# Loading an expert's first layer from memory for each block, in a kernel of polynomial attention and a cosine router

## The chip, the cores and the metric

The kernel runs on one core of a Trainium2 chip. TensorE (PE in the profile, with its weight loads as PEld), VectorE (DVE), ScalarE (ACT), GpSimd (POOL) and SyncE (SP) each work through an instruction list of their own and wait for each other by semaphores. The metric is the device time of one execution in microseconds.

## The reference

Attention without a softmax: queries and keys are turned into 64 features each, and the output is a ratio of two products. Its result, 4352 rows of 128, goes into a router that sends every row to one of 8 experts.

```python
a, b = S1 @ x, S2 @ x                    # 8 numbers each
phi(x) = outer(a, b).reshape(64)
kv = sum over s of phi(k)[f] * v[d];  z = sum over s of phi(k)
x = (phi(q) @ kv) / (phi(q) @ z + 1e-6)  # heads side by side: (4352, 128)

logits = normalised(x) @ normalised(expert_emb).T / tau
expert_idx = argmax(logits);  gate_w = softmax(logits)[expert_idx]
for e in range(8):
    mask = expert_idx == e
    h = maximum(x[mask] @ w1[e], 0)      # 128 -> 1024
    out[mask] = gate_w[mask] * (h @ w2[e])  # 1024 -> 128
```

All is in float32. w1 and w2 have 8 x 128 x 1024 and 8 x 1024 x 128 numbers, 4 MB each.

## The kernel before

The batch of 4 is worked in two halves (m = 0 and 1), each in groups of four token tiles and one last tile. For each group `keys` builds the key features (`tr`, `ab`, `b`, `prod`, `kv`) and `queries` the query features and the output (`tr`, `ab`, `b`, `prod` or `prods`, `tr_qp`, `qpT`, `nd`, `x`); in the first half the query features are kept in `held` until kv is known. `router` finds the best expert of each row (`best`, `pick`), its place among the rows of that expert (`place`, `take`, `split`, `mark`), and writes the rows with their logits to `rows` in memory (`write`, L682 and L686, by SP).

The rows are then worked in blocks of 128 that each have one expert. `plan_early` lays out the first 10 blocks from the counts of the first half, `plan_late` the others from all counts (`count`, `rest`, `shared`, `others`, `experts`); `table` turns places into lists of row numbers (`find`, `high`, `low`, `sums`, `tokens`). Four blocks (30 to 33) have two experts, 64 rows each. 36 blocks are always worked, two more only if a count asks for it (the branch at L1095).

A block i is worked as: `fetch` (POOL gathers its rows, L881), `norm` (ACT squares and sums, POOL takes the root, L949 and L950), `inverse` (DVE, L953 and L954), `turn` (PE transposes the rows, ACT or DVE copies them to xT, L887 and L889), `weights` (the expert's first layer is copied from `w1_sb` to `wb`, L893), `up` (PE, 16 matmul passes, L936, and ACT's relu to hT, L944), `shares` and `share` (the gate, L960, L963, L964), `down` (PE with the second layer, L972 or L975; ACT scales to y, L978; POOL scatters y to the output, L981). Which expert a block has is known only as the program runs: it stands as a number in `exp_i`, an engine loads it into a register (L897), and the address is made from it.

Both layers of all experts are loaded into SBUF by SP: `w1_sb` whole (L181), `w2_sb` for two experts at once and for the others in stages (L176), since its upper half serves as `held`. In w1 as loaded, the 1024 columns stand in the order of memory; the copy to `wb` reorders them so that PE can take 128 at a time.

The order of all work is written out by hand. `put(after, rank, f)` files a step under a tick and a rank, and `emit` issues the steps in that order, on every engine, SP and POOL too. Block i's `up` is in tick first + i (L1061), where first is 10; a step with a lower rank comes sooner in its tick. Buffers rotate: `wb` has four (the tag "rows", shared with the first k and q tiles), xT two, `norm` four, `xs` six, the large PSUM tiles (`ps_big`) two. SP's transfers go by eight semaphores in turn.

POOL is drained once (L1091, ahead of `up` of block 32): it waits there until all that it was given is finished.

Of the kernel before, what the change touches and what calls it, by code (L numbers as in the profile page):

```python
# [19 lines left out]
P = 128  # L20
# [43 lines left out]
def kernel(  # L64
# [113 lines left out]
    LATER = 6  # L178
# [304 lines left out]
    def queries(m, c0, c1, put, put_nd):  # L483
# [52 lines left out]
        def tr_qp():  # L536
            ps = ps_big() if n > 1 else ps_small().rearrange("p (b n) -> p b n", b=2)
            for j in range(n):
# [3 lines left out]
            s["ps"] = ps[:, :, :w]  # L542

        def qpT():
            s["qpT"] = tile_of(n, [P, 2, w], "qpT")
            nc.scalar.copy(s["qpT"], s["ps"])
# [42 lines left out]
        else:  # L589
# [5 lines left out]
                       {tr: (8, 55.3), ab: (8, 84.6), b: (8, 84.7), prod: (9, 20.2), tr_qp: (9, 30.2), qpT: (9, 30.6),  # L595
# [5 lines left out]
        if c1 == s1:  # L601
# [92 lines left out]

    exp_i = [consts.tile([1, n], I32, name=f"exp_i{i}") for i, n in enumerate((EARLY, LATE + SHARED))]

    def blocks(which, upto, weight, place):
# [12 lines left out]

        def experts():
            f = consts.tile([1, n], F32, name=f"exp_f{which}")
            nc.vector.reduce_sum(out=f[:], in_=le[0:1], axis=AX.X)
            nc.vector.tensor_scalar_min(exp_i[which], f, float(E - 1))
        return first, experts
# [60 lines left out]
    def plan_early():  # L776
# [6 lines left out]
        def rest():  # L783
            nc.vector.tensor_tensor_scan(out=upto[:], data0=ones_e[:], data1=full[:], initial=0.0, op0=ALU.mult, op1=ALU.add)
            nc.vector.tensor_scalar(w, full, -1.0, float(KEYS), op0=ALU.mult, op1=ALU.add)
            first, early["experts"] = blocks(0, upto, w, lane)
# [4 lines left out]
        def others():  # L791
            early["experts"]()

# [5 lines left out]
    def plan_late():  # L799
# [12 lines left out]
        def rest():  # L812
# [11 lines left out]
            late["first"], _ = blocks(1, upto, w_late, place)  # L824
# [60 lines left out]
    def turn(i):  # L885
        ps = ps_small()
        nc.tensor.transpose(ps[:, :P], xs[i][:, :DM], ident)  # L887
        xT[i] = w2_sb[:, LATER, 0] if i == 0 else work.tile([P, P], F32, tag="xTb", name="xTb")
        (nc.scalar.copy if i == 0 or 4 <= i <= 8 else nc.vector.tensor_copy)(xT[i], ps[:, :P])  # L889

    def first_layer(to, e, copy=nc.vector.tensor_copy):

        copy(to.rearrange("p (f q) -> p f q", f=NF),  # L893
                              w1_sb[:, bass.ds(e, 1)].rearrange("p o (q f) -> p (o f) q", f=NF))

    def expert(t, j, engine):
        return nc.values_load(exp_i[t][0:1, j:j + 1], engines=(engine,), min_val=0, max_val=E - 1,  # L897
                              skip_runtime_bounds_check_because="a count of experts, clamped to the last one")

    def weights(i):  # L900
        e = expert(*of(i), mybir.EngineType.Activation if i == 0 else mybir.EngineType.DVE)
        wb[i] = rows_p.tile([P, F], F32, tag="rows", name="wb")
        first_layer(wb[i], e, nc.scalar.copy if i == 0 else nc.vector.tensor_copy)
# [11 lines left out]
    def weights_b(i):  # L915
        first_layer(first_b(i), expert(1, LATE + i - FULL, mybir.EngineType.DVE))
# [121 lines left out]
    put(0, 75.5, count)  # L1038
# [17 lines left out]
    def in_ticks(b0, b1, tick):  # L1056
        for i in range(b0, b1 + 1):
# [33 lines left out]
    put_at(first + USUAL - AHEAD)(0, 29.5, lambda: nc.gpsimd.drain(fusable=False))  # L1091
# [42 lines left out]
```

## Time and profile before

| | us |
|---|---|
| median of 3 runs | 212.22 (211.96 to 213.15) |
| the profiled execution | 211.64 |
| its span, first to last instruction | 209.9 |
| PE busy | 194.9 (93% of the span) |
| DVE, ACT, POOL busy | 133.8, 104.0, 118.9 |
| granted TensorE clock | full, in all slices |
| first layer's matmuls start, block 0 | 56.84 |
| the same, blocks 3, 10 and 35 | 74.77, 104.61, 199.96 |
| first gather starts, lands | 52.56, 55.80 |

The profile is of one execution; its sums stand against 211.64, and the 1.7 us around the span are outside of it. A line of the timeline has start and length in us, engine, line of the program, operation, the tile written and those read, and in brackets the idle time of the engine in front of it with whoever ended it. Busy time of PE counts pipelined matmuls with modelled ends.

### The profile page before, as it was taken

To read this page: it belongs to the slowest core of one execution; us is meant where nothing else is said; L and a number is where in the kernel's file an instruction comes from. 1 tells how busy PE (TensorE), PEld (TensorE's weight loads), DVE (VectorE), ACT (ScalarE), POOL (GpSimd) and SP (SyncE) were. 2 spreads that over 40 slices of the span, in tenths; PEclk is the share of its full clock that TensorE was granted. 3 is DMA by queue.
4 is the path that set the end of the run, shared out by engine and by line. 5 is a ranking of instruction groups with operands and counts; after the bars stand their busy time and mean duration, and the time that the engine had idled before them with its cause. 6 is when DMAs were issued, how large, how long until landed. Compare 5 with 4: busy or idle time off the path is not lost.

```text
span 209.9 us, 6913 instructions
## 1 busy us (share of the span) xinstructions
PE 194.9 (93%) x2598; PEld 184.1 (88%) x2598; DVE 133.8 (64%) x441; ACT 104.0 (50%) x292; POOL 118.9 (57%) x134
## 2 busy tenths in 40 slices
PE   8999899989679889999999999999999999999881
PEld 7668798977569889999999999999999999999781
DVE  5867578979877858898536554646464456784220
ACT  2566432353573425652346555454655545777430
POOL 4101000210852757964788888888888888881533
PEclk9999999999999999999999999999999999999999
DMA  4988889998164140100111111111111121110000
GB/s 122 310 209 286 250 294 391 355 384 319 48 179 171 47 128 23 42 16 13 42 41 44 38 39 41 39 41 29 41 33 37 43 41 41 31 40 5 10 25 24
DMA packets 18560, 22.64 MB, mean 108 GB/s; under 512 B 5353, under 2 KB 12788, under 8 KB 18528
## 3 DMA queue, kind: packets, MB, share of 16 engines
q1 hardware_dynamic: 16224, 17.45, 24.8%
q0 software_dynamic: 2304, 4.74, 8.7%
q8 instruction: 22, 0.36, 0.7%
q14 instruction: 10, 0.08, 0.1%
HBM read 17.59 MB, written 4.73 MB: 106 GB/s over the span
## 4 chain that ended last, share of the span: by engine, by line
PE 62%; DVE 17%; issue 8%; POOL 5%; DMA 3%; ACT 2%; DVEq 0%; POOLq 0%
PE ps_big L936 20%; PE ps_acc L972 9%; PE ps_ab L972 9%; PE ps_big L941 4%; PE ps_acc L437 3%; DMA xs<-rows,src_i 3%; PE ps_t L357 2%; POOL out_dram L981 2%; POOL norm L950 2%; PE ps_acc L103 2%; PE ps_t L887 2%; PE ps_acc L975 2%; PE ps_big L554 2%; PE ps_big L520 2%; PE ps_ab L374 2%
## 5 line engine op out<-in xcount | busy, mean ns | idle before, releaser
L981 POOL DMA_INDIRECT out_dram<-y,dst_i x36 | 48.6, 1350 | 29.4 <-ACT sq L949 17.7
L936 PE MATMUL ps_big<-xTb,wb 128*128 128x128 f32 x496 | 61.1, 276 | 3.6 <-DVE xTb L889 1.2
L936 PEld LDWEIGHTS ps_big<-xTb,wb 128*128 128x128 f32 x496 | 57.8, 192 | 4.6 <-issue 3.1
L944 ACT ACTIVATE hT<-ps_big 128x1024 f32<-128x1024 f32 x36 | 36.9, 1024 | 39.9 <-PE ps_big L936 38.8
L881 POOL DMA_INDIRECT xs<-rows,src_i x36 | 39.6, 1100 | 19.5 <-DVE rc L565 9.7
L893 DVE COPY wb<-w_sb 128x1024 f32 x35 | 38.7, 1104 | 12.2 <-issue 11.1
L972 PE MATMUL ps_acc<-w_sb,hT 128*128 x256 | 31.3, 275 | 0.0
L972 PE MATMUL ps_ab<-w_sb,hT 128*128 x256 | 31.2, 275 | 0.0
L972 PEld LDWEIGHTS ps_ab<-w_sb,hT 128*128 128x128 f32 x256 | 29.9, 192 | 0.0
L972 PEld LDWEIGHTS ps_acc<-w_sb,hT 128*128 128x128 f32 x256 | 29.8, 192 | 0.0
L950 POOL TENSOR_TENSOR norm<-norm,half_c 128x1 f32<-128x1 f32 x36 | 25.9, 722 | 2.5 <-ACT sq L949 1.9
L953 DVE TENSOR_SCALAR norm<-norm 128x1 f32<-128x1 f32 x36 | 5.5, 152 | 27.2 <-POOL norm L950 27.1
L960 ACT ACTIVATE probs<-xs,norm 128x8 f32<-128x8 f32 x36 | 10.7, 296 | 7.1 <-DVE norm L954 5.5
L390 POOL TENSOR_TENSOR qp<-both 128x1024 f32<-128x1024 f32 x1 | 2.0, 1958 | 21.4 <-ACT both L385 21.4
L889 DVE COPY xTb<-ps_t 128x128 f32<-128x128 f32 x30 | 8.6, 287 | 6.8 <-PE ps_t L887 6.5
L978 ACT ACTIVATE y<-ps_ab,gate 128x128 f32<-128x128 f32 x18 | 6.6, 366 | 12.7 <-PE ps_ab L972 10.9
L390 DVE TENSOR_TENSOR kp<-ps_ab,kb 128x1024 f32<-128x1024 f32 x8 | 9.7, 1215 | 3.9 <-ACT qpT L529 2.4
L887 PE MATMUL ps_t<-ident,xs 128*128 128x128 f32 x36 | 10.2, 283 | 2.0 <-DMA xs<-rows,src_i 2.0
L978 ACT ACTIVATE y<-ps_acc,gate 128x128 f32<-128x128 f32 x18 | 6.6, 367 | 10.9 <-PE ps_acc L972 8.0
L949 ACT ACTIVATE sq<-xs 128x128 f32<-128x128 f32 x36 | 10.8, 300 | 0.1
L437 PEld LDWEIGHTS ps_acc<-v,kp 128*64 128x64 f32 x256 | 8.1, 138 | 1.8 <-issue 1.7
L437 PE MATMUL ps_acc<-v,kp 128*64 128x64 f32 x256 | 9.2, 225 | 0.3 <-issue 0.3
(241 smaller groups left out, 308.4 us busy)
## 6 DMA issues: line engine op xcount, KB each, us to landing
w_sb<-in_moe_w_dram SPq DMA_DIRECT2D x32, 256.0 KB, 5.7
rows<-xg SPq DMA_DIRECT2D x4, 544.0 KB, 5.0
v<-in_v_dram SPq DMA_DIRECT2D x4, 512.0 KB, 7.2
k<-in_k_dram SPq DMA_DIRECT2D x3, 512.0 KB, 5.2
q<-in_q_dram SPq DMA_DIRECT2D x3, 512.0 KB, 6.4
xs<-rows,src_i POOLq DMA_INDIRECT x36, 2.6
out_dram<-y,dst_i POOLq DMA_INDIRECT x36, 2.3
k<-in_k_dram SPq DMA_DIRECT2D x2, 256.0 KB, 2.9
```

Source lines behind the costliest of these rows:

```text
L390: engine.tensor_mul(t.rearrange("p j h (i k) -> p (j h) i k", i=R), ab[:, :, 0].unsqueeze(3).broadcast_to([P, n * H, R, R]), b.unsqueeze(2 ...
L437: nc.tensor.matmul(acc[m][u * HALF:(u + 1) * HALF, i, p], s["kp"][:, c - c0, h], bass.AP(tensor=vo.tensor, offset=vo.offset, ap=[list(vo.a ...
L881: nc.gpsimd.indirect_dma_start(out=xs[i][:], out_offset=None, in_=rows[:2 * S if t == 0 else N], in_offset=bass.IndirectOffsetOnAxis(ap=sr ...
L887: nc.tensor.transpose(ps[:, :P], xs[i][:, :DM], ident)
L893: copy(to.rearrange("p (f q) -> p f q", f=NF), w1_sb[:, bass.ds(e, 1)].rearrange("p o (q f) -> p (o f) q", f=NF))
L936: nc.tensor.matmul(ps[:, u, j * P:(j + 1) * P], w[:, f * P:(f + 1) * P], x, start=True, stop=True)
L944: nc.scalar.activation(hT[i], ps, ACT.Relu)
L949: nc.scalar.activation(sq, xs[i][:, :DM], ACT.Square, accum_out=norms[i])
L950: nc.gpsimd.tensor_tensor(out=norms[i], in0=norms[i], in1=half_c, op=ALU.pow)
L972: nc.tensor.matmul(ps, h[:, f * P:(f + 1) * P], ws[0][:, f], start=f == 0, stop=f == NF - 1)
L978: nc.scalar.activation(y, ps, ACT.Copy, scale=gate.pop(i)[:, 0:1])
L981: d = nc.gpsimd.indirect_dma_start(out=out[:, :], out_offset=bass.IndirectOffsetOnAxis(ap=dst_i[t][:, j:j + 1], axis=0), in_=y[:], in_offs ...
```

## The change

`w1_sb` is gone. `first_layer` now loads the expert's whole first layer, 128 rows of 4 KB, from memory into `wb` (or into the free halves of `v_flat` for the second expert of a block) by SP, with the expert's number in a register of SP. There is no copy, on DVE or, for block 0, on ACT; columns come in memory's order, and w2 is loaded in the matching order ("(f p) d" for "(p f) d"), in pieces of 512 bytes where it was 2048. All of w2 is loaded at once behind the attention's inputs, since `held` is a tile of its own.

The number of block 0's expert is made first and alone (`expert_0`, into `exp_0`), the other nine in a later tick. The transposes of one query group are issued in two halves, with `turn(0)` between them. `norm` is issued three blocks ahead where it was two, with six buffers; that of block 0 stands ahead of its `up`, that of the last block ahead of the drain. The late counts, and with them the place of the last group's rows, stand behind `up` of block 3 where they stood ahead of it. POOL is drained once more, in the middle of the blocks (before `up` of block 18).

```diff
-    w1_sb = consts.tile([P, E, F], F32, name="w1_sb")
-    held = w2_sb[:, E // 2:].rearrange("p e f d -> p e (f d)")
+    held = consts.tile([P, E // 2, F], F32, name="held")
     def load_w2(e):
         for u in range(2):
-            nc.sync.dma_start(w2_sb[:, e, f], w2[e].rearrange("(p f) d -> p f d", p=P)[:, f])
+            nc.sync.dma_start(w2_sb[:, e, f], w2[e].rearrange("(f p) d -> p f d", p=P)[:, f])
     for e in range(E):
-        for u in range(2):
-            nc.sync.dma_start(w1_sb[:, e, u * F // 2:(u + 1) * F // 2], w1[e, :, u * F // 2:(u + 1) * F // 2])
-    for e in range(2):
         load_w2(e)
...
-                       {..., tr_qp: (9, 30.2), qpT: (9, 30.6),
+                       {..., (lambda: tr_qp(0)): (9, 30.2), (lambda: tr_qp(1)): (9, 30.22), qpT: (9, 30.6),
...
-                at_rank = {best: (1, 31), pick: (1, 31), place: (1, 75.1), take: (1, 76), split: (1, 76),
+                at_rank = {best: (1, 31), pick: (1, 31), place: (2, 31), take: (2, 32), split: (2, 32),
...
+        def expert_0():
+            nc.vector.reduce_sum(out=f[:], in_=le[0:1], axis=AX.X)
+            nc.vector.tensor_scalar_min(exp_0, f[:, 0:1], float(E - 1))
         def experts():
-            nc.vector.reduce_sum(out=f[:], in_=le[0:1], axis=AX.X)
             nc.vector.tensor_scalar_min(exp_i[which], f, float(E - 1))
...
-    def first_layer(to, e, copy=nc.vector.tensor_copy):
-        copy(to.rearrange("p (f q) -> p f q", f=NF),
-                              w1_sb[:, bass.ds(e, 1)].rearrange("p o (q f) -> p (o f) q", f=NF))
+    def first_layer(to, t, j):
+        e = expert(t, j, mybir.EngineType.SP)
+        nc.sync.dma_start(to, w1[bass.ds(e, 1)].rearrange("o p f -> (o p) f"))
...
-        norms[i] = work.tile([P, 1], F32, tag="norm", bufs=4, name="norm")
+        norms[i] = work.tile([P, 1], F32, tag="norm", bufs=6, name="norm")
...
-    for e in range(2, LATER):
-        put_at(ND_AT[0][-1])(0, 55.5 if e < 4 else 83, lambda e=e: load_w2(e))
-    for e in range(LATER, E):
-        put_at(ND_AT[0][-1])(3, 30.1, lambda e=e: load_w2(e))
...
+    put(0, 62.2, lambda: early["expert_0"]())
+    put(1, 21, lambda: early["experts"]())
-    put(1, 30.1, lambda: turn(0))
+    put(1, 30.21, lambda: turn(0))
...
-    put(0, 75.5, count)
+    put(1, 31.5, count)
...
-                known_by = i - (1 if EARLY <= i <= known + AHEAD else 2) - b0
-                to = put_at(tick + max(known_by, 0))
-                to(*((0, 46) if i == b0 else (0, 74.6)), lambda i=i: norm(i))
-                to(*((0, 59) if i == b0 else (1, 46)), lambda i=i: inverse(i))
+                t = max(i - (1 if EARLY <= i <= known + AHEAD else 3), b0)
+                to = put_at(tick + t - b0)
+                if i == 0:
+                    put(-1, 30.7, lambda: norm(0))
+                    put(0, 59, lambda: inverse(0))
+                else:
+                    to(0, 46 if i == b0 else 29.2 if i == USUAL - 1 else 74.6, lambda i=i: norm(i))
+                    to(*((1, 46) if i > t else (0, 59)), lambda i=i: inverse(i))
...
-    put_at(first + USUAL - AHEAD)(0, 29.5, lambda: nc.gpsimd.drain(fusable=False))
+    for t in (USUAL // 2, USUAL - AHEAD):
+        put_at(first + t)(0, 29.5, lambda: nc.gpsimd.drain(fusable=False))
```

More of the change, by code (lines that the diff above doesn't have):

```diff
@@ L175, in load_w2 @@
             f = slice(u * NF // 2, (u + 1) * NF // 2)
-            nc.sync.dma_start(w2_sb[:, e, f], w2[e].rearrange("(p f) d -> p f d", p=P)[:, f])
-    LATER = 6
+            nc.sync.dma_start(w2_sb[:, e, f], w2[e].rearrange("(f p) d -> p f d", p=P)[:, f])
     for e in range(E):
-        for u in range(2):
-            nc.sync.dma_start(w1_sb[:, e, u * F // 2:(u + 1) * F // 2], w1[e, :, u * F // 2:(u + 1) * F // 2])
-    for e in range(2):
         load_w2(e)
@@ L534, in prods, with tr_qp @@
                                  s["b"][:, j].rearrange("p (j a n) -> p j a n", j=2, a=2))
-        def tr_qp():
-            ps = ps_big() if n > 1 else ps_small().rearrange("p (b n) -> p b n", b=2)
-            for j in range(n):
+        def tr_qp(half=None):
+            if half != 1:
+                s["ps"] = ps_big() if n > 1 else ps_small().rearrange("p (b n) -> p b n", b=2)
+            ps = s["ps"]
+            for j in range(n) if half is None else range(2 * half, 2 * half + 2):
                 for p in range(2):
@@ L541, in tr_qp @@
                                         s["qp"][:, j, 2 * p:2 * p + 2].rearrange("p h f -> p (h f)"), ident)
-            s["ps"] = ps[:, :, :w]
         def qpT():
             s["qpT"] = tile_of(n, [P, 2, w], "qpT")
-            nc.scalar.copy(s["qpT"], s["ps"])
+            nc.scalar.copy(s["qpT"], s["ps"][:, :, :w])
         def nd():
@@ L594, in queries @@
                         nd: (9, 30), x: (9, 71)},
-                       {tr: (8, 55.3), ab: (8, 84.6), b: (8, 84.7), prod: (9, 20.2), tr_qp: (9, 30.2), qpT: (9, 30.6),
+                       {tr: (8, 55.3), ab: (8, 84.6), b: (8, 84.7), prod: (9, 20.2), (lambda: tr_qp(0)): (9, 30.2),
+                        (lambda: tr_qp(1)): (9, 30.22), qpT: (9, 30.6),
                         nd: (10, 70), x: (10, 71)},
@@ L693 @@
     dst_i = [consts.tile([P, n], I32, name=f"dst_i{i}") for i, n in enumerate(SIZES)]
+    exp_0 = consts.tile([1, 1], I32, name="exp_0")
     exp_i = [consts.tile([1, n], I32, name=f"exp_i{i}") for i, n in enumerate((EARLY, LATE + SHARED))]
@@ L709, in first @@
             return at
+        f = consts.tile([1, n], F32, name=f"exp_f{which}")
+        def expert_0():
+            nc.vector.reduce_sum(out=f[:], in_=le[0:1], axis=AX.X)
+            nc.vector.tensor_scalar_min(exp_0, f[:, 0:1], float(E - 1))
         def experts():
-            f = consts.tile([1, n], F32, name=f"exp_f{which}")
-            nc.vector.reduce_sum(out=f[:], in_=le[0:1], axis=AX.X)
             nc.vector.tensor_scalar_min(exp_i[which], f, float(E - 1))
-        return first, experts
+        return first, expert_0, experts
     def column(name, dt=F32, w=E):
@@ L785, in rest @@
             nc.vector.tensor_scalar(w, full, -1.0, float(KEYS), op0=ALU.mult, op1=ALU.add)
-            first, early["experts"] = blocks(0, upto, w, lane)
+            first, early["expert_0"], early["experts"] = blocks(0, upto, w, lane)
             at = first()
@@ L791, in others @@
         def others():
-            early["experts"]()
             nc.vector.tensor_scalar_min(c_early[:, 1:], upto, float(EARLY))
@@ L823, in rest @@
             nc.vector.tensor_add(place[:, PAIRS:PAIRS + SHARED], place[:, PAIRS:PAIRS + SHARED], s["high"])
-            late["first"], _ = blocks(1, upto, w_late, place)
+            late["first"], _, _ = blocks(1, upto, w_late, place)
         def shared():
@@ L887, in turn @@
         nc.tensor.transpose(ps[:, :P], xs[i][:, :DM], ident)
-        xT[i] = w2_sb[:, LATER, 0] if i == 0 else work.tile([P, P], F32, tag="xTb", name="xTb")
+        xT[i] = work.tile([P, P], F32, tag="xTb", name="xTb")
         (nc.scalar.copy if i == 0 or 4 <= i <= 8 else nc.vector.tensor_copy)(xT[i], ps[:, :P])
-    def first_layer(to, e, copy=nc.vector.tensor_copy):
-        copy(to.rearrange("p (f q) -> p f q", f=NF),
-                              w1_sb[:, bass.ds(e, 1)].rearrange("p o (q f) -> p (o f) q", f=NF))
     def expert(t, j, engine):
-        return nc.values_load(exp_i[t][0:1, j:j + 1], engines=(engine,), min_val=0, max_val=E - 1,
+        number = exp_0[:, 0:1] if t == j == 0 else exp_i[t][0:1, j:j + 1]
+        return nc.values_load(number, engines=(engine,), min_val=0, max_val=E - 1,
                               skip_runtime_bounds_check_because="a count of experts, clamped to the last one")
+    def first_layer(to, t, j):
+        e = expert(t, j, mybir.EngineType.SP)
+        nc.sync.dma_start(to, w1[bass.ds(e, 1)].rearrange("o p f -> (o p) f"))
     def weights(i):
-        e = expert(*of(i), mybir.EngineType.Activation if i == 0 else mybir.EngineType.DVE)
         wb[i] = rows_p.tile([P, F], F32, tag="rows", name="wb")
-        first_layer(wb[i], e, nc.scalar.copy if i == 0 else nc.vector.tensor_copy)
+        first_layer(wb[i], *of(i))
     def second_layer(t, j):
@@ L915, in weights_b @@
     def weights_b(i):
-        first_layer(first_b(i), expert(1, LATE + i - FULL, mybir.EngineType.DVE))
+        first_layer(first_b(i), 1, LATE + i - FULL)
     def second_b(i):
```

## The prediction

> **What bounds the kernel now.** I read the 40 slices first, then busy times by window, then the chain of waits and the timeline where TensorE (PE) has holes.
>
> The slices: a digit is the busy tenths of 5.25 us.
>
> ```profile
> PE   8999899989679889999999999999999999999881
> ...
> DMA  4988889998164140100111111111111121110000
> ```
>
> PE is full except around slices 11 to 15, 18 to 20 and the end; DMA is full until 50 us and nearly empty afterwards. By window (start:end, length, then busy us of PE, its weight loads, DVE, ACT, POOL):
>
> ```profile
> 50.00:55.00 5.00, 3.61 (x69) 3.13 (x67) 4.51 (x17) 3.01 (x2) 2.13 (x2) 1.00 0.43 152
> 55.00:60.00 5.00, 4.20 (x58) 4.03 (x58) 3.93 (x7) 2.71 (x7) 3.55 (x4) 1.00 0.20 48
> 60.00:65.00 5.00, 3.83 (x41) 3.35 (x39) 3.58 (x16) 2.73 (x11) 2.64 (x4) 1.00 0.88 293
> 70.00:75.00 5.00, 3.33 (x47) 3.08 (x46) 4.15 (x20) 1.96 (x6) 4.48 (x6) 1.00 0.43 149
> ...
> 115.00:190.00 75.00, 75.00 (x835) 74.31 (x835) 43.15 (x131) 42.55 (x126) 63.89 (x63) 1.00 0.15 38
> ```
>
> From 105 to 195 us PE never idles: a block costs 1.79 (first layer) + 1.79 (second) + about 0.1 = 3.69 us, and nothing there can gain. The holes are 1.39 + 0.80 + 1.17 + 1.67 us in these windows, 0.85 between 90 and 105, and one at the end. Who ended them (start, length, in brackets the idle time and its releaser):
>
> ```profile
> 55.80 0.33 PE L887 MATMUL ps_t<-ident,xs 128*128 128x128 f32 x1 [1.82 <-DMA xs<-rows,src_i]
> 60.83 0.15 DVE L953 TENSOR_SCALAR norm<-norm 128x1 f32<-128x1 f32 x1 [0.68 <-POOL norm L950]
> 62.61 2.02 PE L936 MATMUL ps_big<-xTb,wb 128*128 128x128 f32 x16 [1.17 <-DVE parts L570]
> 74.77 2.02 PE L936 MATMUL ps_big<-xTb,wb 128*128 128x128 f32 x16 [0.96 <-DVE place_k L669]
> 93.88 2.02 PE L936 MATMUL ps_big<-xTb,wb 128*128 128x128 f32 x16 [0.32 <-DVE wb L893]
> 96.29 2.17 PE L748 MATMUL ps_t<-col,row 128*128 128x64 bf16 x34 [0.38 <-DVE col L742]
> 197.69 0.15 DVE L953 TENSOR_SCALAR norm<-norm 128x1 f32<-128x1 f32 x1 [4.47 <-POOL norm L950]
> 199.96 2.05 PE L936 MATMUL ps_big<-xTb,wb 128*128 128x128 f32 x16 [1.19 <-DVE xTb L889]
> ```
>
> Nearly all are PE behind DVE, and DVE behind its copies or behind POOL's norm. The groups that the change touches:
>
> ```profile
> L893 DVE COPY wb<-w_sb 128x1024 f32 x35 | 38.7, 1104 | 12.2 <-issue 11.1
> L981 POOL DMA_INDIRECT out_dram<-y,dst_i x36 | 48.6, 1350 | 29.4 <-ACT sq L949 17.7
> L950 POOL TENSOR_TENSOR norm<-norm,half_c 128x1 f32<-128x1 f32 x36 | 25.9, 722 | 2.5 <-ACT sq L949 1.9
> ```
>
> **What the Trainium skill says.** "SBUF — State Buffer", section "SBUF: two separate sides": DMA ports and engine ports don't contend, while GpSimd and some DVE operations lock each other out for a whole instruction. The trace agrees on the lock: the norm at 70.32 lasts 1.45 us and ends at 71.77, just behind the copy at 70.64 (1.10); a free one takes 0.58. An output scatter takes 1.49 us over a copy and 1.02 clear of one. "DMA: Bandwidth & Descriptors", section "Specifications", gives 512 B as the least transfer for line rate; the trace's packet records have 27 ns for 512 B and 84 ns for 2048 B, on 16 engines 303 against 390 GB/s. Its section "Latency and other measured facts" gives a register load about 600 ns; the trace has 0.70 (DVE, 64.60) and 0.51 (POOL, 206.03).
>
> **Copies out, loads in.** 39 DVE copies go (35 for wb, 4 for v; 38.7 + 4.4 us) with 0.33 to 0.88 us of register load before each, and one ACT copy (2.09). In their place SP issues 40 loads of 512 KB (36 blocks, 4 second halves). Transfer: 4096-byte packets are not in this queue's trace; between 84 ns for 2048 and 168 for 4352 I take 160, so 8 packets an engine are 1.3 us of 3.69. Time to landing: the 544 KB row writes at 63.29 and 72.18, in a quiet queue, took 2.76 and 3.24; with register load (0.7) and issue (0.5) I take 4.3 us, bounds 3.5 and 8.3 (the worst landing of a 512 KB load in the busy queue). Cover: wb has 4 buffers, so load i+4 may start when up(i) ends and is needed 3 x 3.69 + 1.84 = 12.9 us later. The four second halves have two buffers: 6.2 us. Both hide 4.3; nothing is charged. If the cover went, each load would cost its excess. On SP's queue the late row writes now stand behind loads: the third behind those of blocks 1 and 2, whose number is there at 54.8 and whose buffers are free, the fourth behind that of block 4, which waits for up(0); both are through before the write's own data (near 61.9 and 68). The loads share the 16 engines with POOL's gathers, which run four blocks ahead: a burst of 1.3 us before one of them doesn't reach PE.
>
> **The first load** has no such cover. exp_0 is ready right behind col, 49.23 + 0.38 = 49.6; load landed at 53.9 (bounds 53 to 58). It stands on SP behind all second-layer loads and the first two row writes (issued by 45), which no longer wait for PE to free a tile.
>
> **Early DMA.** Second layers: 4 MB in 512 B packets, 16 x 0.86 = 13.8 us at 303 GB/s behind the last query load (landed 30.4), done at 44.2; the first loads of this packet size averaged 234 GB/s over 2.6 to 7.1, which gives 17.9 us and 48.3. Before, w1 and half of w2 kept the row write issued at 44.03 until 51.16. Now it lands near 48 (or 51.7). The first gather started at 52.56, with its indices done at 51.14; indices move to 51.35 (0.38 of exp_0 ahead of qp, part of it hidden by PE's sums until 50.5), and 0.8 us of POOL overhead, the gap at 99.09 to 99.89, gives 52.15: 0.4 gained, bounds -0.4 and 1.
>
> **up(0).** Rows land at 52.15 + 3.24 = 55.4. PE does half of the eight transposes (0.5) before it needs them, then xs, then the other half: 56.15. The PSUM bank frees when DVE's parts ends: 56.2 (55.85 plus 0.1 for exp_0 and 0.2 for the exp_i now there). So 56.25 against 56.84: 0.6 gained. If the first load is later than 56.2, it decides instead.
>
> **up(1).** ACT's qpT moves from 57.10 to 56.2; qb, qp, xTb(1) follow, DVE 59.35. The norm of block 0, now ahead of hT on ACT and behind the fourth gather on POOL, is ready at 58.75, so DVE doesn't wait until 60.83; parts waits for PE's nd (58.3 to 59.6) and ends at 61.1, 1.4 earlier; up(1) at 61.2. Queued behind: the copies at 65.47 and 70.64 are gone, so PE runs through to the end of down(1), 9.6 us as before: 70.8.
>
> **up(3).** It now stands ahead of the late counts (place, 0.8 us of PE). xTb(3) is there at 69.7, bank at 67.4, wb(3) at 66.5. So up(3) 70.8, counts to 73.4, up(4) at 75.4 against 78.53: 3.1 gained. The register load before up(3), bare before, hides behind down(1).
>
> **Late table.** DVE's planning after the counts starts at 73.55 (73.89 before), no sooner than PE needs, but five copies of 1.43 us fewer. I followed it to col: done at 92.1, up(8) ends at 92.2. So the 0.48 before up(8) and 0.55 before the sums go: 3.1 + 0.48 + 0.55 = 4.1 at the sums. The wait for the late gather before turn(10) stays, since its indices follow the sums; I take 3.9 at up(10), 0.2 less for hand-overs that I rounded.
>
> **Tail.** POOL's drain (187.49 to 195.11) delays norm(34), hence the 4.47 and PE's wait before up(35): 199.96 against 198.65 if PE had run on. Both last norms now stand ahead of it: 1.3 gained. The end still hangs 3.9 us behind the last y.
>
> **Second drain.** Mid-loop, bounds 1.3 (last drain) and 5.6 us (this one, from the norm's end). It starts behind a gather, about 3.4 us after up(18) starts; a scatter and a norm follow (2.1), and DVE's inverse may come up to 6.4 after the start of up(19), 10.1 after that of up(18), before the next xTb is late. So 4.6 us of drain are free and 5.6 would cost 1; I take 0, since fewer transfers lie before it. POOL then catches up: its round of 3.57 us (gathers at 141.56 and 145.13) loses the 0.47 of the scatter that copies lengthen. Squares, now three blocks ahead, need their gather a block sooner: issued 3.4 us into the block before, landing 2.9 later, needed 7.8 into it.
>
> **Sum.** 3.9 + 1.3 = 5.2. Profiled execution: 211.64 us for a span of 209.9, so 206.4; the median shown is 0.58 above it: 207.0.
>
> **Rivals.** (B) Early data late: w2 at 234 GB/s or the first load beyond 56.2 gives back 1 to 2.5 us: 208.5. For: 512 B packets never ran long here. Against: 1.7 us of slack. (C) The mid drain, or POOL's lateness behind it, holds DVE: 1 to 1.5 us, 208.3. (D) Slower: loads land later than 12.9 us behind their buffer's release, at PE's wait before up(i); four loads are in flight, so each run of four blocks adds the excess, 34 / 4 = 8.5 times. 0.6 us of excess eats the gain, 1.2 gives 207.0 + 10.2 = 217. Against: 20 MB in 135 us is 148 GB/s on a queue that did 390. (E) The copies were hidden anyway: only tail and counts remain, 210.5.
>
> **Numbers.** A 0.55 (alone 206.0 to 208.0), B 0.22, C 0.08, D 0.07, E 0.08. Range 205.3 (all holes gone, 5.9 + 1) to 210.2. A measurement here tells about 0.5% (1.1 us) from no change: faster 0.88, same 0.05, slower 0.07.
>
> **What shows it.** No L893 copies; scatters near 1.02 us; up(0) near 56.3, up(4) near 75.4, up(10) near 100.7; PE's wait in front of up(35) gone; a POOL drain in mid-loop without a PE hole. Wrong if PE waits for a wb load anywhere, above all at up(0), or if row writes land after 51.4.

## The result and the profile after

| | before | after |
|---|---|---|
| median of 20 runs each, us | 213.77 (211.64 to 216.46) | 211.03 (209.56 to 213.60) |
| ratio after / before | | 0.9884, 95% interval 0.9859 to 0.9909 |
| the profiled execution, its span | 211.64, 209.9 | 211.84, 210.1 |

The change makes the kernel 1.2% faster, about 2.5 us, where 2.5% and 5.2 us were forecast. The ratios here and below leave disturbed executions out and the medians do not, so a ratio can differ from that of its medians, by 0.7 to 0.9% in e4 and e11. Before's longer series lies 1.5 us above the three runs that the forecast had; its profiled execution is the fastest of its 20, while the profiled one of after lies above its median. So the two traces differ by +0.2 us where the medians differ by -2.7, and the traces are read below for where time went, not for the total.

The slices of after's page (one is 5.25 us; PEclk is the granted TensorE clock):

```profile
PE   8999898989699999998899999997999999999991
...
PEclk9999999999999999999699999999999999999999
DMA  5976999992548586209546647454466787285000
```

PE has lost its holes (stretches in which it has nothing to do) in slices 12 to 15 and keeps the one in slice 11. New are one at slices 19 and 20, followed by a lower clock, and one at slice 28, in the middle of the blocks. DMA is no longer empty after 50 us.

The windows of after (start:end, length, busy us of PE, its weight loads, DVE, ACT, POOL, then clock, DMA share, GB/s):

```profile
50.00:55.00 5.00, 4.37 (x78) 3.80 (x77) 4.76 (x15) 1.01 (x1) 2.59 (x3) 1.00 0.44 125
55.00:60.00 5.00, 3.73 (x42) 3.14 (x41) 2.64 (x6) 2.44 (x7) 2.17 (x4) 1.00 0.77 233
60.00:65.00 5.00, 4.71 (x67) 4.24 (x65) 4.46 (x21) 3.73 (x12) 3.45 (x5) 1.00 0.34 126
70.00:75.00 5.00, 5.00 (x65) 4.99 (x64) 2.17 (x12) 3.15 (x9) 3.84 (x6) 1.00 0.72 210
95.00:100.00 5.00, 3.90 (x34) 3.58 (x32) 1.44 (x10) 1.37 (x3) 2.93 (x3) 1.00 0.98 324
100.00:105.00 5.00, 4.22 (x23) 4.22 (x24) 0.52 (x3) 0.75 (x5) 1.98 (x2) 0.66 0.48 159
115.00:190.00 75.00, 73.83 (x810) 72.94 (x808) 16.93 (x98) 40.55 (x121) 52.27 (x60) 1.00 0.61 194
```

DVE's load in the block stretch fell from 43.15 to 16.93 us, and of the holes at 60 and 70 us one is small now (0.29 us) and one gone. New are 95 to 105: DMA full at 324 GB/s, PE idle for 1.1 us, then 23 matmuls where there is time for 45. In 115 to 190 PE lost 1.17 us where before it lost none.

The timeline of after, PE's lines at these places (start, length, and in brackets the idle time ahead with its releaser):

```profile
56.60 0.33 PE L887 MATMUL ps_t<-ident,xs 128*128 128x128 f32 x1 [1.27 <-DMA xs<-rows,src_i]
62.29 2.02 PE L935 MATMUL ps_big<-xTb,wb 128*128 128x128 f32 x16 [0.29 <-PE ps_t L537]
...
100.78 0.33 PE L887 MATMUL ps_t<-ident,xs 128*128 128x128 f32 x1 [1.88 <-DMA xs<-rows,src_i]
100.95 3.57 PE L971 MATMUL ps_acc<-w_sb,hT 128*128 x16
...
104.31 2.04 PE L935 MATMUL ps_big<-xTb,wb 128*128 128x128 f32 x16
...
146.15 2.05 PE L935 MATMUL ps_big<-xTb,wb 128*128 128x128 f32 x16 [1.09 <-DVE xTb L889]
...
200.17 2.05 PE L935 MATMUL ps_big<-xTb,wb 128*128 128x128 f32 x16
```

The waits behind DVE's copies of first layers are gone, and of those behind POOL's norms one is left, a new one: the copy to xT ahead of 146.15 stands behind a norm that the mid drain made late (e1). What PE waits for most now is the gather, twice: ahead of turn(0) at 56.60 and of turn(10) at 100.78. And down(8) at 100.95 takes 3.57 us; its 16 passes took 1.95 elsewhere.

The groups of after that answer to the copies, scatters and norms, and the gathers' time from issue to landing (the last number; before it was 2.6):

```profile
L980 POOL DMA_INDIRECT out_dram<-y,dst_i x36 | 37.5, 1043 | 43.8 <-ACT y L977 17.2 <-ACT sq L948 12.5 <-issue 7.7
L949 POOL TENSOR_TENSOR norm<-norm,half_c 128x1 f32<-128x1 f32 x36 | 21.6, 606 | 6.8 <-ACT sq L948 6.5
```

```profile
xs<-rows,src_i POOLq DMA_INDIRECT x36, 4.0
```

Side by side, with what the prediction's steps said (start in us; a dash where they give none; those of up(21) and up(35) are its gains of 3.9 and 5.2 us taken from before):

| | before | predicted | after |
|---|---|---|---|
| first gather issued | 52.56 | 52.15 | 51.80 |
| up(0) | 56.84 | 56.25 | 57.34 |
| up(1) | 62.61 | 61.2 | 62.29 |
| up(4) | 78.53 | 75.4 | 76.19 |
| sums | 96.29 | 92.2 | 92.71 |
| turn(10) | 102.62 | - | 100.78 |
| up(10) | 104.61 | 100.7 | 104.31 |
| up(21) | 145.21 | 141.3 | 146.15 |
| up(34) | 194.72 | - | 196.18 |
| up(35) | 199.96 | 194.8 | 200.17 |

Of 3.58 us gained at the sums, 0.30 is left twelve microseconds later, at up(10): turn(10) comes 8.07 us behind the sums where it was 6.33 (1.74 lost), and up(10) 3.53 behind turn(10) where it was 1.99 (1.54 lost). Then 1.24 go at up(21), 0.52 between it and up(34), which no run was made for, and 1.25 come back at up(35).

### The profile page after: what moved, and what is told of

The parts are those of the page before. It is cut to its first block, busy times and chain, and to the rows that moved or that the text cites. A ratio compares the mean times of both kernels' runs of the same rounds, so it can differ in the third digit from the quotient of the medians.

```text
span 210.1 us, 6984 instructions
## 1 busy us (share of the span) xinstructions
PE 196.7 (94%) x2598; PEld 185.6 (88%) x2598; DVE 93.7 (45%) x403; ACT 101.8 (48%) x291; POOL 101.3 (48%) x134
## 4 chain that ended last, share of the span: by engine, by line
PE 68%; issue 13%; DVE 7%; DMA 4%; POOL 4%; POOLq 1%; ACT 1%; ACTq 0%
PE ps_big L935 22%; PE ps_acc L971 12%; PE ps_ab L971 10%; DMA xs<-rows,src_i 4%; PE ps_acc L432 3%; PE ps_t L352 3%; PE ps_big L550 3%; PE ps_big L515 2%; POOL out_dram L980 2%; PE ps_acc L103 2%; PE ps_ab L369 2%; PE ps_big L940 2%; PE ps_t L887 2%; POOL xs L881 1%; PE ps_acc L974 1%
## 5 line engine op out<-in xcount | busy, mean ns | idle before, releaser
L935 PE MATMUL ps_big<-xTb,wb 128*128 128x128 f32 x512 | 63.0, 276 | 1.4 <-DVE xTb L889 1.1
L935 PEld LDWEIGHTS ps_big<-xTb,wb 128*128 128x128 f32 x512 | 59.9, 192 | 2.3 <-DVE xTb L889 1.3
L980 POOL DMA_INDIRECT out_dram<-y,dst_i x36 | 37.5, 1043 | 43.8 <-ACT y L977 17.2
L881 POOL DMA_INDIRECT xs<-rows,src_i x36 | 36.3, 1008 | 17.9 <-issue 8.4
L971 PE MATMUL ps_acc<-w_sb,hT 128*128 x256 | 32.9, 284 | 0.0
L971 PEld LDWEIGHTS ps_acc<-w_sb,hT 128*128 128x128 f32 x256 | 31.4, 200 | 0.0
L949 POOL TENSOR_TENSOR norm<-norm,half_c 128x1 f32<-128x1 f32 x36 | 21.6, 606 | 6.8 <-ACT sq L948 6.5
L962 DVE TENSOR_SCALAR gate<-gate 128x1 f32<-128x1 f32 x36 | 5.3, 148 | 16.5 <-ACT probs L959 16.4
```

The source lines that it names most:

```text
L881: nc.gpsimd.indirect_dma_start(out=xs[i][:], out_offset=None, in_=rows[:2 * S if t == 0 else N], in_offset=bass.IndirectOffsetOnAxis(ap=sr ...
L935: nc.tensor.matmul(ps[:, u, j * P:(j + 1) * P], w[:, f * P:(f + 1) * P], x, start=True, stop=True)
L949: nc.gpsimd.tensor_tensor(out=norms[i], in0=norms[i], in1=half_c, op=ALU.pow)
L971: nc.tensor.matmul(ps, h[:, f * P:(f + 1) * P], ws[0][:, f], start=f == 0, stop=f == NF - 1)
L980: d = nc.gpsimd.indirect_dma_start(out=out[:, :], out_offset=bass.IndirectOffsetOnAxis(ap=dst_i[t][:, j:j + 1], axis=0), in_=y[:], in_offs ...
```

## The experiments

Three suspects came out of the trace: the late gather(10) with the lower clock behind it, the new drain in the middle of the blocks (the mid drain), and the late gather(0). Times are medians; "before" is the kernel before on the same chip and in the same series.

| | us | before | ratio, 95% interval |
|---|---|---|---|
| e1 no mid drain | 209.55 | 213.20 | 0.9835, 0.9783 to 0.9887 |
| e2 gather(10) first | 208.37 | 213.20 | 0.9768, 0.9703 to 0.9834 |
| e3 shifted fetch | 222.68 | 213.20 | 1.0434, 1.0374 to 1.0494 |
| e4 loads alone | 213.60 | 213.20 | 0.9935, 0.9900 to 0.9971 |
| e5 split loads | 208.73 | 214.78 | 0.9741, 0.9633 to 0.9849 |
| e6 turn(10) behind down(8) | 209.51 | 214.78 | 0.9797, 0.9705 to 0.9890 |
| e7 more early instructions | 211.68 | 214.78 | none formed |
| e8 two fixes | 207.32 | 214.78 | 0.9689, 0.9594 to 0.9785 |
| e9 three edits | 213.44 | 220.59 | 0.9678, 0.9590 to 0.9765 |
| e10 rest alone | 222.06 | 220.59 | none formed |
| e11 counts back | 217.12 | 220.59 | 0.9916, 0.9866 to 0.9965 |

### e1: the mid drain

```diff
-    for t in (USUAL // 2, USUAL - AHEAD):
+    for t in (USUAL - AHEAD,):
         put_at(first + t)(0, 29.5, lambda: nc.gpsimd.drain(fusable=False))
```

> The changed kernel without the drain ahead of block 18; the last drain stays. Theory (the drain holds POOL for 6.15 us from 137.50, block 20's norm comes late, DVE's inverse with it, and PE waits 1.09 us before up(21)): that hole is gone and the kernel takes about 1.1 us less than the changed kernel, ratio to before near 0.983. Rival (POOL or its gathers would be late there anyway, since transfers now stand in front of them): a hole of about the same size appears elsewhere between blocks 18 and 24, ratio stays at 0.988.

The timeline of the changed kernel, POOL around the drain:

```profile
136.49 1.01 POOL L881 DMA_INDIRECT xs<-rows,src_i  x1 [0.17 <-issue]
143.65 1.02 POOL L980 DMA_INDIRECT out_dram<-y,dst_i  x1 [6.15 <-issue]
144.67 0.60 POOL L949 TENSOR_TENSOR norm<-norm,half_c 128x1 f32<-128x1 f32 x1
```

POOL stands for 6.15 us behind a gather that itself needs 4.58 to land, then does a scatter and the norm; DVE's inverse starts at 145.31, xT is copied at 145.83, and up(21) begins at 146.15. In e1, up(20) and up(21) are:

```profile
142.49 1.95 PE L935 MATMUL ps_big<-xTb,wb 128*128 128x128 f32 x16
146.17 1.95 PE L935 MATMUL ps_big<-xTb,wb 128*128 128x128 f32 x16
```

There is no hole: up(21) follows up(20) by 3.68 us where it was 4.93. The ratio moved from 0.9884 to 0.9835, the expected value, but the two intervals overlap, so the size of the gain rests on the traces. From up(10) to up(32) they have 83.32 us in the change and 83.16 in e2, which has the drain; 82.17 in e1 and 81.87 in e8, which have it not. (In e1 PE stands for 1.34 us inside up(32), with no releaser named, far from the blocks of the rival.) So in the change the drain costs 1.1 to 1.3 us, as the theory had it; it need not, as e3 and e7 show below.

### e2: block 10's number made first

exp_10 holds the number of block 10; those of the later blocks are made behind the late lists, so the loads for blocks 11 and 12 are released later.

```diff
-            nc.vector.tensor_scalar_min(exp_i[1], f, float(E - 1))
+            nc.vector.tensor_scalar_min(exp_10, f[:, 0:1], float(E - 1))
...
+    put(6, 75.3, lambda: late["experts_rest"]())
...
-        number = exp_0[:, 0:1] if t == j == 0 else exp_i[t][0:1, j:j + 1]
+        number = (exp_0, exp_10)[t][:, 0:1] if j == 0 else exp_i[t][0:1, j:j + 1]
```

> The changed kernel with the expert's number of block 10 made alone and those of the later blocks made behind the late lists, so that of the first-layer loads only block 10's stands ahead of the first late gather; those of blocks 11 and 12 follow it. Theory (three loads of 512 KB released together fill the DMA queues from 94 to 99.6 and gather(10), issued at 96.31, moves its first packet only at 99.66): gather(10) lands 2.7 to 3.1 us after its issue and not 4.4, PE's wait before turn(10) shrinks from 1.88 to 0.3 us or less, up(10) starts at 102 to 103, 1.5 us earlier or more (3 us where the granted clock also stays full); ratio near 0.982. Rival (the gather is slow on its own, by the 28 blocks' list or POOL): landing stays above 4, ratio 0.988.

The timelines at the same place, first the changed kernel, then e2 (there, lines of the code are 6 higher). A row of SPq stands for several loads, x5 for five, and starts with the first:

```profile
93.72 12.99 SPq L898 DMA_DIRECT2D wb<-in_moe_w_dram  x5
...
96.31 1.01 POOL L881 DMA_INDIRECT xs<-rows,src_i  x1 [2.82 <-issue]
```

```profile
96.53 1.01 POOL L887 DMA_INDIRECT xs<-rows,src_i  x1 [2.83 <-issue]
...
98.37 5.06 SPq L904 DMA_DIRECT2D wb<-in_moe_w_dram  x4
...
99.14 0.33 PE L893 MATMUL ps_t<-ident,xs 128*128 128x128 f32 x1
99.31 1.98 PE L977 MATMUL ps_acc<-w_sb,hT 128*128 x16
101.12 1.95 PE L941 MATMUL ps_big<-xTb,wb 128*128 128x128 f32 x16
```

In the change the loads of blocks 10, 11 and 12 were issued at 93.72, 94.61 and 95.53, since all numbers were there at once, and gather(10) came 0.8 us behind the last. With two of the three out of its way turn(10) starts 2.61 us behind the gather's issue (4.47 in the change), PE does not wait, the clock stays full, and up(10) is 3.2 us earlier than in the change. The ratio fell to 0.9768, with an interval that does not meet that of the change, and all six executions have a mean clock of 0.998 or more. The theory holds; the rival's landing above 4 us did not come (2.56 us).

### e5: the same loads in smaller pieces

```diff
-        nc.sync.dma_start(to, w1[bass.ds(e, 1)].rearrange("o p f -> (o p) f"))
+        n = P // parts
+        for r in range(0, P, n):
+            nc.sync.dma_start(to[r:r + n], w1[bass.ds(e, 1), r:r + n].rearrange("o p f -> (o p) f"))
```

> The changed kernel with each first-layer load of a block with one expert issued as four of 32 rows (128 KB); register loads, order and everything else as in the change. Theory (a gather waits in each DMA engine for the whole share, eight 4 KB rows, of the 512 KB load that stands there, about 1.3 to 1.6 us; two rows are a quarter of that): the first part of gather(10) lands 2.5 to 2.9 us after its issue and not 3.93, the last below 3.7 us and not at 4.43, PE's wait before turn(10) falls from 1.88 to 1.0 us or less and the granted clock stays full; ratio 0.978 to 0.984. Rival (a gather stands behind all loads that were issued before it, whatever their pieces, or SP's four issues hold the loads back): first part still at 3.5 us or later, PE's wait as before or longer, ratio 0.988 or above.

The timeline of e5:

```profile
95.87 1.01 POOL L881 DMA_INDIRECT xs<-rows,src_i  x1 [2.83 <-issue]
...
99.36 0.33 PE L887 MATMUL ps_t<-ident,xs 128*128 128x128 f32 x1 [0.90 <-DMA xs<-rows,src_i]
```

The semaphore's sixteen updates, one from each DMA engine, came 2.80 to 3.45 us behind the issue; in the change they came at 3.93 to 4.43, in before at 2.34 to 2.69. So smaller pieces help, but this run does not say why, since it changes two things at once. SP needs 0.5 us or more for every piece: when gather(10) was issued at 95.87, only the four quarters of block 10's load (512 KB) were ahead of it, and three quarters of block 11's followed before its first packet moved. In the change all three loads were ahead, and 1480 of their 1536 KB had begun to move before the gather's first packet at 99.66.

One reading is that a gather waits for one share of a load in each DMA engine. The Trainium skill, "DMA: Bandwidth & Descriptors", section "Queues, rings and completion order", says that each engine takes turns between queues and finishes a whole packet of one before it turns to the next. A 512 KB load gives each engine eight rows of 4 KB, in this trace 159 ns each (median), an estimate of 1.27 us in all if the eight are one such packet, which no record shows. The first updates fit that size: 1.6 us of delay in the change, about 0.5 with quarters. The other reading, the rival's, is that the gather waits for whatever was issued ahead, and in e5 that was less. It fits as well, and a run with the same bytes ahead in smaller pieces was not made.

Over the gathers whose sixteen updates are all in the record, the median landing went only from 3.95 us (33 gathers) to 3.61 (30), and the first part of a gather came later, 2.87 us behind the issue for 2.56. The ratio, 0.9741, is below the expected 0.978 to 0.984, with an interval that covers these; in its trace the hole before up(21) was smaller as well, 0.61 us.

### e6: PE's order, and the clock

```diff
-                put(0, 45, lambda i=i: turn(i + 1))
+                put(0, 74.5 if i + 1 == EARLY else 45, lambda i=i: turn(i + 1))
```

> The changed kernel with one step moved on PE: the transposes of block 10's rows (turn(10)) stand behind down(8), whose input is ready long before, and not ahead of it. The loads and the gather's lateness stay. Theory (the hole of 1.88 us ahead of turn(10) is 55% of one of the 3.413 us stretches at whose ends the granted clock changes, and that is why the clock is halved for the next stretch, in which down(8) takes 3.57 us and not 1.95): down(8) fills the hole, the idle share stays below 0.5, the clock stays full, and up(10) starts near 101.5 and not 104.31; ratio 0.976 to 0.980. Rival (the clock is granted by something else, such as the load on the memory or the chip): it drops at the same place with PE busy, up(10) comes at 102.5 or later, ratio 0.983 or above.

The timeline of e6:

```profile
98.22 1.95 PE L971 MATMUL ps_acc<-w_sb,hT 128*128 x16
...
101.94 0.33 PE L887 MATMUL ps_t<-ident,xs 128*128 128x128 f32 x1 [1.77 <-DMA xs<-rows,src_i]
102.65 3.68 PE L935 MATMUL ps_big<-xTb,wb 128*128 128x128 f32 x16 [0.38 <-DVE xTb L889]
```

In this one profile the gather landed 6.1 us behind its issue, so a hole stayed behind down(8), and the clock was halved again, now under up(10). As an experiment on the hole this profile is a miss. The other four executions have a mean clock of 0.997 to 1.0 and took 209.42 to 209.93 us, where a whole halved stretch would make it 0.992, but no trace says when the gather landed in them. All five together are at 0.9797 of before, 1.8 us below the change, and the two intervals overlap: what the order is worth is not shown.

What goes ahead of a halved clock can be read from all profiles together. The record of the clock changes only at multiples of 3.413 us: in the change full for 95.573 (28 of them), half for one, full for 31. I laid these stretches over each trace and took the share of each without a matmul or weight load. Here are all of 0.43 or more, the last two stretches of each span left out:

```
idle share of a stretch   the next stretch's clock
0.43  e2, e10, e11        full
0.50  e7                  full
0.53  before (at 53.0)    full
0.55  after, e8           half
0.60  e3                  half
0.63  e6                  half
0.64  e7                  half
0.65  e10 (twice)         half
0.78, 0.79  e1, e4        half
0.83, 0.94  e9, e11       half
```

Eleven stretches with 0.55 or more were all followed by a halved one. Below that only one was, in e10: a stretch that was halved itself, with 0.28 idle. The Trainium skill, "TensorE: Matmul & The Clock Gate", part 1, describes just such fixed stretches of 3413 ns that don't start with the kernel. Its section "Why this matters for your kernels" allows gaps of up to about 3 us; here one of 1.88 us, which happened to lie inside one stretch (97.7 to 101.1), was enough, and down(8) behind it took 1.6 us more. Where the page and these traces differ, the traces decide. Whether a hole is charged twice thus depends on where it falls: e2's of 1.98 us ahead of turn(0) was split between two stretches (0.43) and cost only itself, e8's of 1.84 was not. The second charge does not fall on every execution: the ten of after's twenty with a mean clock of 0.992 or less have a median of 211.2 us, the other ten one of 210.7.

### e3 and e7: the last part of gather(0)

In after, fifteen of gather(0)'s sixteen parts landed 2.55 to 3.09 us behind the issue and the last at 4.75. A 16 KB instruction transfer (54.45, 0.93 us) ran in between. In before, of the 33 gathers whose sixteen updates are all in the record, 13 have an instruction transfer of 8 or 16 KB begin during them; the last part lags by more than 0.2 us in 8 of these and in none of the 20 others; in the change it lags in 16 of 21 and in 2 of 12.

```diff
 e3
-        for _ in range(n):
-            nc.tensor.matmul(ps_warm[:, :P], zeros, zeros, start=True, stop=True)
+        for _ in range(4 * n):
+            nc.tensor.matmul(ps_warm[:, :P // 4], zeros, zeros[:, :P // 4], start=True, stop=True)
 e7
-    for _ in range(7):
+    for _ in range(36):
...
-    keep_warm(9)
+    keep_warm(4)
```

> The changed kernel with the nine warm-up matmuls at the start, which compute nothing that is used, cut into 36 of a quarter of the width each: PE has about a hundred instructions more in its list in about the same time, so its instructions are fetched some 4 us earlier from there on. Theory (the last of gather(0)'s sixteen parts, 1.66 us behind the fifteenth, was held by a 16 KB instruction transfer at 54.45 in the same DMA engine): the fetch falls elsewhere, the sixteenth part follows the fifteenth within 0.3 us, turn(0) starts at 55.3 and up(0) near 56.1, in the profile 1 us or more earlier than 57.34; of that 0 to 1 us is left at up(10). Rival (block 0's load, running until 53.9, holds the part): the sixteenth part still lags by more than 1 us and up(0) stays at 57.3.

> The changed kernel with other warm-up matmuls at the start, which compute nothing that is used: 36 tiny ones for 7 and 4 wide ones for 9, some hundred PE instructions more in about the same time, so that PE's instruction transfers come some 4 us earlier. Theory (one of these 16 KB transfers, begun 2 to 3 us behind the issue of gather(0), is what holds that gather's last part in the profiles where it lags): none falls into gather(0), PE's wait before turn(0) is below 0.5 us, up(0) follows the start of the last query product (line 550 of the changed kernel, first time) by 9.4 us and not 10.6, and 1 us of it is left at the sums; ratio 0.982 to 0.986. Rival (block 0's load holds it): up(0) 10.6 us behind, ratio 0.988.

e3 is slow by the edit itself: a matmul pass of 32 columns took nearly as long as one of 128, 72 passes in 15.57 us where 18 had taken 4.15, and everything starts 12 us later. Its profile can be read all the same: no transfer within gather(0), last part at 3.19, up(0) 9.43 us behind the first query product (10.60 in the change). e7 took the same time at the start, its transfer came before the gather's parts, and up(0) followed by 9.42 us. Its median, 211.68, is 0.986 of before's, but its four times go from 208.26 to 212.97, so that no gain can be told; by its profile PE stood for 2.18 us at 33.5 with no releaser named, and gather(10) was 2.93 us late. So the moved transfer went with a punctual gather, as the theory says, but that is no proof: in e1, e4, e5 and e6 a transfer did begin during gather(0), and up(0) followed by 9.42 or 9.43 us all the same. Of the profiles with loads, the gather was late in after, e2 and e8 alone. Which DMA engine the transfer takes is not in the records; with block 0's load ending 0.4 to 1.1 us ahead of it in every one of these, the two causes are not told apart. This stays open. Its price is not: 1.17 us at up(0) in the change, and 2.0 in e8, where the clock is halved behind it and takes 1.17 more (up(1) comes 6.12 us behind up(0), in the change 4.95):

```profile
56.59 0.35 PE L893 MATMUL ps_t<-ident,xs 128*128 128x128 f32 x1 [1.84 <-DMA xs<-rows,src_i]
...
57.59 3.19 PE L941 MATMUL ps_big<-xTb,wb 128*128 128x128 f32 x16
```

The two runs show one thing more, about the mid drain, which both still have. The gather that it waits for is gather(22). In ten profiles (all but e3, e7 and e9, whose record lacks updates) a 16 KB transfer begins in its time, and its last part lags by 0.6 to 1.6 us; in e3 and e7 no transfer begins there, the lag is 0.05 and 0.12, and the gather lands at 3.13 and 2.98 us where the change had 4.58. POOL then stands for 4.70 and 4.55 us where it stood for 6.15, and up(21) follows up(20) by 3.68 us: no hole. In the change, e2, e5, e6 and e11, POOL's stand less what up(21) lost is 4.9 us each time (6.15 less 1.24 in the change). So that much is free, and the price of the drain is what its gather's last part adds to it.

### e4, e10, e11: which part gave the gain

e4 is before with the loads; e10 is before with all the rest of the change; e11 is the change with the counts put back:

```diff
 e11
-                at_rank = {best: (1, 31), pick: (1, 31), place: (2, 31), take: (2, 32), split: (2, 32),
+                at_rank = {best: (1, 31), pick: (1, 31), place: (1, 75.1), take: (1, 76), split: (1, 76),
...
-    put(1, 31.5, count)
+    put(0, 75.5, count)
```

> The kernel before with only the loads of the change (no copies, first layers loaded per block, second layers loaded at once and in the other layout, block 0's number first); norms, late counts, drain and transposes as before. Theory (the copies were mostly hidden: the gain to block 9 came from the counts' new place, and that at the end from the norms ahead of the drain): no more than 1 us below before, ratio 0.995 to 1.003, with PE's holes before up(3) and before up(35) still there. Rival (DVE's copies held PE through the late table): 2 us or more below before, ratio 0.990 or less.

> The kernel before with everything of the change but the loads: norms three blocks ahead, block 0's and the last one's moved, late counts behind up(3), the query transposes in two halves with turn(0) between, the second drain; copies and w1 in SBUF as before. Theory (loads alone gave 0.65% less, the whole change 1.2% less; the rest gives up(1) 0.9 us, the last norms 1.3 us and loses 1.1 us or more to the mid drain): 1 us below before, ratio 0.993 to 0.998. Rival (the counts' new place gives 2 us or more on its own, as the prediction had it): ratio 0.990 or less, up(4) at 76.5 or earlier.

> The changed kernel with the late counts and the place of the last group's rows back ahead of up(3). Theory (the counts made PE wait only because copies kept DVE back; without copies their place is worth 0.3 us): up(4) follows up(1) by 14.2 us where the change has 13.9, no hole of 0.5 us before up(3), ratio 0.987 to 0.992. Rival (the place is worth 1.5 us or more): holes before the counts and before up(3) come back, up(4) 15.5 us or more behind up(1), ratio 0.995 or above.

From up(1) to up(4) the traces have 15.92 us in before, 14.17 in e4, 15.63 in e10, 14.13 in e11 and 13.90 in the change. So taking the copies out is worth 1.75 us there, the counts' place 0.2 to 0.3, with copies or without. In e4 the holes before up(3) and before up(35), which I expected to stay, are gone (up(35) follows up(34) by 3.99 us as in the change, 5.24 before): e4's theory fell, and the copies were not hidden. Nor was the ratio 2 us better, as the rival had it: 0.9935. The gain at the sums, 3.18 us, was there, and turn(10) waited 2.71 us with a halved clock behind it, so that up(10) came 0.72 us later than in before.

e10 shows no gain over before (219.07 to 222.74 us against 216.41 to 222.91), where 1 us was expected; with four executions no ratio was formed. Its timeline shows a loss:

```profile
149.49 1.02 POOL L983 DMA_INDIRECT out_dram<-y,dst_i  x1 [5.06 <-ACT hT L946]
...
152.08 1.08 DVE L895 COPY wb<-w_sb 128x1024 f32 x1 [0.33 <-issue]
...
153.08 0.28 DVE L891 COPY xTb<-ps_t 128x128 f32<-128x128 f32 x1
...
153.42 2.72 PE L938 MATMUL ps_big<-xTb,wb 128*128 128x128 f32 x16 [3.27 <-DVE xTb L891]
```

The drain is shorter here, but behind the late norm DVE has a copy to make before xT, and the hole is 3.27 us where it is 1.09 with loads; the clock is halved for a stretch behind it. The two parts of the change are not a sum: with the copies still there, the hole behind the mid drain is three times as long. By the traces the rest, put on top of e4's loads, is worth next to nothing (0.84 at up(1) and 0.25 at the counts, less 1.24 at the drain), while the ratios of e4 and of the change differ by 0.5%. All of e4's 22 executions have a mean clock of 0.997 or less, against 12 of after's 20, so halved stretches may make up the difference; that was not tried.

All three profiles of that series (e9, e10, e11) also have PE idle for 2.6 to 3.3 us right ahead of up(0), behind other engines (DVE's parts in e9, ACT's qpT in e11, ACT's qb in e10), with turn(0) punctual but in e10; on that chip before took 220.59. No other profile shows it, e10 has no loads, and the cause is not known.

### e8 and e9: together

e8 is e1's and e2's edits, e9 those and e5's.

> The changed kernel without the drain ahead of block 18 and with block 10's number made ahead of the others, so that both the mid-loop hole (1.09 us) and the late gather(10) are gone. Theory (the two losses lie one behind the other on PE's path and add up): about 1 us below the second of them alone, 207.2 us where before has 213.2, ratio 0.970 to 0.974. Rival (POOL needs the time elsewhere; the losses overlap): ratio stays at 0.977.

> The changed kernel with all three edits of the earlier runs: no drain ahead of block 18, block 10's number ahead of the others, first-layer loads of blocks with one expert in four parts. Theory (what split loads gain is the gathers' waiting, which the two other edits leave at turn(0) alone): PE's wait before turn(0) below 0.5 us, no hole of 0.5 us or more from block 0 to block 35, ratio 0.964 to 0.969. Rival (the gain of the split loads was that of gather(10) alone, and that is had already): the same as with the two edits, 0.969 to 0.972.

e8 is the fastest against before, 0.9689: 3.1% where the change has 1.2, and the intervals of the two don't meet. The ratio is a little below the expected 0.970 to 0.974. Its interval covers the rival's 0.977 too, but by the trace the losses do add up: there is no wait at turn(10) and none at up(21), and what is left is the late gather(0) with the halved clock shown above. e9, 0.9678, is no better than e8 as far as can be told. That is what the rival says, that the gain of splitting was that of gather(10) and e8 has it already; but e9 ran on another chip, with the unexplained hole ahead of up(0), so the rival is not shown either.

## Why the prediction was right or wrong

- **Readings of before.** One is wrong: PE's digits at slices 18 to 20 are all 9, and the 0.85 us of holes there come from the windows and the timeline alone. Nor is DMA nearly empty right behind 50 us (slices 12, 13 and 15 have 6, 4 and 4 tenths). No step rests on either.
- **First load, early data.** exp_0 was ready at 49.89 (49.6), load 0's last packet came at 53.92 (53.9). The second layers had landed at 46.55, between 44.2 and 48.3; the row write at 49.20, between 48 and 51.7; the first gather started at 51.80, between the bounds. Rival B did not occur.
- **up(0)** came 1.1 us later than forecast. The step "Rows land at 52.15 + 3.24" failed: they took 4.75 us, for a cause that stays open (e3 and e7). Where the gather is punctual, up(0) is 9.43 behind the first query product, here 56.17, and the step's 56.25 is right.
- **up(1)** at 4.95 us behind up(0), forecast 4.95; with the norm ahead of hT, 0.84 less than in e4, which leaves it where it was (5.79), and in before (5.77).
- **up(4)** at 13.90 behind up(1), forecast 14.2. The forecast named the counts' place beside the copies; the runs give 1.75 of it to the copies.
- **Late table.** 3.58 us gained at the sums, forecast 4.1, with up(0) 1.1 us late from the start: behind up(0) the step gained more than it said.
- **Loads.** Landing 4.1 us (4.3); PE waits for none in after's trace. Rival D is excluded, and scatters are at 1043 ns (1.02 us).
- **The steps that failed.** First, in "Copies out, loads in": "a burst of 1.3 us before one of them doesn't reach PE", because gathers run four blocks ahead. Those at the head of a list have no such lead: gather(0) and gather(10) start when their indices are made, with PE waiting, and gather(10) met the loads. "Late table" even said that the wait before turn(10) stays, and took it as it was in before, where the gather landed in 2.69 us. The forecast did not ask what else the same moment releases: three loads whose numbers come out of one step on DVE. The gather took 4.43 us. In the profile that cost 1.74 us, and through the clock, which no step had, 1.54; e2, where one load was ahead of it, has neither loss.
- **Second drain**, taken as 0 "since fewer transfers lie before it". It lasted 6.15 us, above the bound of 5.6, since its gather took 4.58 us to land; up(21) lost 1.24 us. This step failed too, by the size of the drain: the 4.6 us called free were 4.9, and with gather(22) punctual (e3, e7) the drain does cost nothing. Rival C had the mechanism and the size (1 to 1.5), with 0.08 as its chance.
- **Tail.** 1.25 us, forecast 1.3. The step is right, but either part of the change is enough for it: up(35) follows up(34) by 3.99 us in e10, with the norms moved and the copies kept, and in e4, with the copies gone and the norms where they were. In before it was 5.24.

At up(10) the forecast had 3.9 us gained, and in the profiled pair 0.3 was there. With e2's edit it is 3.5, with gather(0) late all the same. So the gains up to the sums were forecast well, and what was missing are costs that the loads and the drain brought with them. The median, 211.03, lies above the range of 205.3 to 210.2. Part of that is the baseline: before's own median lies 1.5 us above the three runs that the range was counted from. The gain of 2.5 us for 5.2 does not hang on it.

## What to carry to other kernels

Where copies are replaced by loads, look for the transfers that the engines wait for at once, with no blocks of lead, and count what is released at the same moment on other queues: let the load that is needed first go alone, with the awaited transfer behind it, or cut the loads into pieces. By these traces a hole in PE of more than half of 3.4 us may be charged twice. And a full stop of one engine costs what the slack behind it leaves, so price it with the transfers that will be under way in the new kernel, not with those of the old one.

## What the hardware showed that was not expected

- The clock, from the stretches above: at full clock, halved for the next stretch of 3.413 us behind any that was idle for 0.55 or more of its length, never at 0.53 or less, in thirteen profiles with the last two stretches of each left out; 10 of after's 20 executions have a mean clock of 0.992 or less, and one halved stretch in 208 us is 0.992.
- Instruction transfers of 16 KB (22 in after, 0.96 us each in the median) stand beside the data: in before all 8 gathers whose last part lags by more than 0.2 us (up to 1.88) had one, or one of 8 KB, begin in its time, and in the change 16 of 18. Moving these transfers by other instructions at the start (e3, e7) went with a punctual gather(22).
- A matmul pass of 32 columns with a full weight load took 15.57 / 72 = 0.22 us in the first microseconds of e3, nearly as much as one of 128 columns (4.15 / 18 = 0.23).
